# Earlier loads of the weight blocks in an attention-then-FFN kernel, with the squares in buffers of their own

## The chip, the core and the metric

The kernel runs on one core of a Trainium2 chip. The core has five engines that run their own instruction streams in order: TensorE (PE, with its weight loads shown as PEld), VectorE (DVE), ScalarE (ACT), GpSimd (POOL) and SyncE (SP), which here does nothing but issue DMAs. The metric is the device time of one execution in microseconds. The kernel before the change takes 992.15 us (median of three runs, 991.67 to 992.97).

## What is computed

Windowed causal attention with a linear bias, 8 batches of 8 heads, 576 positions, head size 64, window 128. Its output is the input of a bilinear feed-forward network with 512 model and 1536 hidden columns:

```
scores = scale * q @ k.T + bias        # only 0 <= i - j < 128 is kept
attn   = softmax(scores)
x      = (attn @ v), heads side by side  # 4608 x 512
out    = ((x @ w_a) * (x @ w_b)) @ w_out
```

All operands are float32, and the weights arrive as 64-bit words: the kernel takes them apart itself and turns each weight into a pair of float16 (high and low part), so that the large products run as three float16 products.

## The kernel before

**Stages.** Attention of batch 0 comes first (`first_attention`), in float32 and with the work on the weights woven in. Then, for each batch b, the feed-forward products of batch b ("up", lines 856 and 867 to 916; "down", lines 818 and 952) are woven with the attention of batch b+1 (`attention`, a generator that `Pace` advances). For batch 0 the functions are `first_up` and `first_down` (PE lines 856 and 818). Work on pairs of heads is called p0 to p3; the chain of a pair is scores (L380 or L384 on PE, L388 on DVE, L389 on ACT; in batch 0 L576, L587, L588), normalised probabilities `phl` (L405, L406), a transposing DMA into `pT` (L411; one buffer), and the product with v (L507).

**The weights.** 18 blocks pass through three places for raw data, `raws[n % 3]`, which lie in the storage of `wdn` (so the profile names them `wdn`). A block holds two slices: blocks 0 to 11 one of w_a and one of w_b, blocks 12 to 17 two of w_out. `load_weights` issues two DMAs of 512 KB on SP. `convert(n)` is three instructions on DVE that read the raw place and write the float32 form (L132, L134, L135; the form is named `wsum`). `squares(n)` is one ACT instruction (L141) that reads the form and writes the squares as bfloat16 **into the raw place of the same block**. For blocks 0 to 11 four matmuls on PE sum these squares (`up_norms`, L157, tile `wn_ps`), a reduction on DVE (L162) and three small POOL steps make the scales for two blocks, and `split_up` writes the float16 pairs `wup` (L149 on ACT, L150 on DVE). For blocks 12 to 17 ACT adds up the squares itself; when all six are done, L223, L102, one matmul (`wtot`, L103) and a few small steps make `ratio` (L227), with which L231 and L232 write the float16 pairs `wdn` over the raw places. A place can be loaded again only when the squares in it have been read, so `up_weights` puts the load of block f+3 behind the matmuls of block f, one turn of its loop after the conversion, and `down_weights` puts it behind the squares.

**What sets the order.** Python generators are advanced against each other: `other(...)` in `first_attention`, and `weave` in `first_batch`. That gives the order of the source; for PE, DVE, ACT and POOL a list scheduler then reorders up to the end of batch 0, by its own estimate of when operands are ready. SP's order is that of the source ("manual schedule"). From batch 1 on PE's order is that of the source too. On SP every DMA stands behind all that were issued before it: in `first_batch` the load of v for batch 1 (`load_v`, L273) waits until the last reader of v of batch 0 (L442) is done, and everything behind it on SP waits as well.

**Buffers that the change uses.** The pool `work` holds the tags "qk" (one buffer, 128 x 1152 float32) and "qst" (one buffer, 128 x 1152 float16). Both are first used for batch 2, by the loads at L316 and L317 and by L352 and L353.

## Time and profile before

| what | us |
|---|---|
| median of three runs (lowest, highest) | 992.15 (991.67, 992.97) |
| the profiled execution, its own time | 989.81 |
| the span of the profiled execution | 988.0 |
| PE busy in the span | 962.1 (97%) |
| DVE busy / ACT busy / POOL busy | 669.0 / 635.6 / 255.3 |

A row of the timeline begins with its start and its duration, both in us; durations overlap a little with the next row's start, because a row ends with the last write. Rows of the waits give the total, the number of times and the longest. The table of stretches gives, for each engine, the busy time and the number of instructions, then the granted PE clock, the share of the DMA engines and the rate.

### The profile page before, as it was taken

The page shows a single profiled execution, that of the slowest core. Times are in us where ns is not written, and L with a number is a line of the kernel's source. Part 1 is how long each engine was busy: PE and PEld are TensorE (multiplying, and loading weights), DVE is VectorE, ACT ScalarE, POOL GpSimd, SP SyncE. Part 2 cuts the span into 40 slices and gives each one's busy share as a digit, 9 for nine tenths or more (in the row PEclk, how much of TensorE's full clock was granted, in tenths as well). Part 3 has the DMA queues.
Part 4 walks back from the last instruction along what each step waited for, and adds up shares of the span by engine and source line. Part 5 has one row for each costly group of instructions (what it writes and reads, how often), then busy time and mean ns, then how long its engine had stood idle before and what let it go on. Part 6 is the DMA issues. An engine that isn't in the chain of part 4 may idle for free.

```text
span 988.0 us, 23867 instructions
## 1 busy us (share of the span) xinstructions
PE 962.1 (97%) x9339; PEld 748.9 (76%) x9339; DVE 669.0 (68%) x1867; ACT 635.6 (64%) x1729; POOL 255.3 (26%) x309
## 2 busy tenths in 40 slices
PE   7899999999999999999999999999999999999998
PEld 5567777677777777777777777777777777877776
DVE  5979998668688657777778677757776576514520
ACT  5977769667676667766767766777667766413321
POOL 1211122032546313541225222211232012311100
PEclk8999999999999999999999999999999999999999
DMA  8434753664337234463345362373245432200001
GB/s 333 168 126 172 231 154 67 151 158 92 80 74 183 68 69 87 107 172 75 68 92 121 120 118 65 87 191 84 59 84 117 133 74 38 55 34 5 1 13 36
DMA packets 148432, 102.82 MB, mean 104 GB/s; under 512 B 120032, under 2 KB 128352, under 8 KB 147296
## 3 DMA queue, kind: packets, MB, share of 16 engines
q1 hardware_dynamic: 138816, 91.77, 38.2%
q10 hardware_dynamic: 9504, 9.54, 3.0%
q8 instruction: 73, 1.20, 0.5%
q14 instruction: 39, 0.32, 0.1%
HBM read 48.33 MB, written 9.44 MB: 58 GB/s over the span
## 4 chain that ended last, share of the span: by engine, by line
PE 69%; DVE 12%; ACT 7%; DMA 7%; issue 3%; POOL 1%; SPq 0%; ACTq 0%; DVEq 0%
PE ch L856 19%; PE dn_ps L952 18%; PE p L856 14%; PE up_ps L856 9%; PE x_ps L507 4%; DMA v<-in_vP 4%; PE sc_ps L384 3%; DVE phl L406 2%; PE dn_ps L818 2%; ACT t L389 1%; DVE wsum L135 1%; DVE xs L442 1%; ACT phl L405 1%; DVE wsum L134 1%; DMA qk<-in_kT 1%
## 5 line engine op out<-in xcount | busy, mean ns | idle before, releaser
L856 PEld LDWEIGHTS <-wup 128*128 128x128 f16 x3072 | 296.3, 98 | 82.0 <-issue 5.7
L952 PE MATMUL dn_ps<-h,wdn 128*128 128x288 f16 x2016 | 254.4, 286 | 0.0
L952 PEld LDWEIGHTS <-wdn 128*128 128x128 f16 x2016 | 193.9, 98 | 52.0 <-issue 0.2
L856 PE MATMUL up_ps<-xs,wup 128*128 128x288 f16 x1536 | 194.6, 286 | 1.1 <-ACT rc L867 0.8
L856 PEld LDWEIGHTS <-wsum 128*128 128x128 f16 x1152 | 111.7, 98 | 32.0 <-issue 2.5
L911 POOL TENSOR_TENSOR rc<-rc,row 128x288 f32<-128x288 f32 x64 | 62.3, 974 | 279.8 <-DVE row L909 263.9
L389 ACT ACTIVATE t<-t,mn 128x192 f32<-128x192 f32 (+2 forms) x252 | 107.2, 427 | 24.5 <-DVE mn L388 24.4
L856 PE MATMUL ch<-xs,wup 128*128 128x288 f16 x768 | 115.0, 286 | 0.5 <-ACT row L893 0.5
L856 PE MATMUL p<-xs,wup 128*128 128x288 f16 x768 | 115.1, 286 | 0.0
L406 DVE SCALAR_TENSOR_TENSOR phl<-t,rin,phl 128x192 f16<-128x192 f32 (+2 forms) x252 | 104.6, 454 | 15.3 <-ACT phl L405 15.1
L856 PE MATMUL ch<-xs,wsum 128*128 128x288 f16 x768 | 111.5, 286 | 1.1 <-ACT rc L881 1.1
L848 ACT CAST h<-rc 128x576 f16<-128x576 f32 x96 | 64.1, 668 | 69.1 <-DVE rc L916 37.2
L405 ACT ACTIVATE phl<-t,rin 128x192 f16<-128x192 f32 (+2 forms) x252 | 88.9, 425 | 25.3 <-DMA pT<-phl 12.7
L849 DVE TENSOR_TENSOR h<-rc,h 128x576 f16<-128x576 f32 x90 | 69.5, 772 | 30.5 <-ACT h L848 29.7
L388 DVE CUSTOM_DVE_ANT_0 t<-sc_ps,bias,neg 128x192 f32<-128x192 f32 (+2 forms) x216 | 73.9, 389 | 7.6 <-PE sc_ps L384 7.5
L957 ACT ACTIVATE row<-dn_ps,oi 128x288 f32<-128x288 f32 x56 | 27.6, 493 | 55.9 <-PE dn_ps L952 55.9
L893 ACT ACTIVATE row<-ch,g 128x288 f32<-128x288 f32 x64 | 31.8, 497 | 48.9 <-PE ch L856 48.9
L442 DVE TENSOR_TENSOR xs<-v,xs 128x576 f16<-128x576 f32 x52 | 47.8, 935 | 21.4 <-ACT xs L441 21.3
L888 DVE TENSOR_TENSOR rc<-p,rc 128x288 f32<-128x288 f32 x64 | 29.1, 454 | 44.3 <-PE p L856 34.7
L365 POOL TENSOR_SCALAR bias<-rel_sb,ninv,sl_sb 128x192 f32<-128x192 f32 x24 | 20.0, 832 | 147.8 <-DVE mn L388 129.8
L856 PE MATMUL p<-xs,wsum 128*128 128x288 f16 x384 | 57.5, 286 | 0.0
L436 POOL TENSOR_TENSOR xq<-xq,sq 128x576 bf16<-128x576 bf16 x22 | 29.2, 1325 | 75.7 <-ACT sq L435 75.7
(155 smaller groups left out, 1386.1 us busy)
## 6 DMA issues: line engine op xcount, KB each, us to landing
v<-in_vP SPq DMA_DIRECT2D x8, 1280.0 KB, 6.2
out<-row ACTq DMA_DIRECT2D x62, 144.0 KB, 1.8
qk<-in_qT SPq DMA_DIRECT2D x28, 288.0 KB, 4.0
qk<-in_kT SPq DMA_DIRECT2D x28, 288.0 KB, 4.4
wdn<-in_w_a SPq DMA_DIRECT2D x12, 512.0 KB, 5.1
wdn<-in_w_b SPq DMA_DIRECT2D x12, 512.0 KB, 6.1
wdn<-in_w_out SPq DMA_DIRECT2D x12, 512.0 KB, 4.6
qst<-qkh SPq DMA_DIRECT2D x24, 144.0 KB, 2.7
```

Source lines behind the costliest of these rows:

```text
L388: vec.tensor_tensor_reduce(out=t[:, c:c + w], in0=ps[:, c:c + w], in1=o.bias[:, WIN - w:WIN], scale=-0.125 if o.b == 1 else o.neg, scalar= ...
L389: act.activation(t[:, c:c + w], t[:, c:c + w], AF.Exp, bias=o.mn[:, n:n + 1], scale=-1.0, accum_out=o.sm[:, n:n + 1])
L405: act.activation(phl[:, 0, pc:pc + w], e, AF.Copy, scale=s)
L406: vec.scalar_tensor_tensor(out=phl[:, 1, pc:pc + w], in0=e, scalar=s, in1=phl[:, 0, pc:pc + w], op0=ALU.mult, op1=ALU.subtract)
L442: vec.tensor_tensor(out=xs[:, n, 1, :, :], in0=src, in1=xs[:, n, 0, :, :], op=ALU.subtract)
L507: last = pe.matmul(xp[oc // 512][64 * h:64 * h + 64, o0:o0 + w], vt[0:rows, c:c + 64], probs(pt, rows, blocks, h), start=(n == 0 and first ...
L848: act.copy(h[:, f, :, 0, :], hid)
L849: eng.tensor_tensor(out=h[:, f, :, 1, :], in0=hid, in1=h[:, f, :, 0, :], op=ALU.subtract)
L856: pe.matmul(ps[:, 0:HT], w[:, wi, k, :], xs[:, b, xi, k, :], start=(first and n == 0), stop=(last and n == len(ks) - 1), skip_group_check= ...
L893: last_read[0] = last_main[0] = act.activation(mid, ch, AF.Copy, scale=st.g)
L911: pool.tensor_tensor(out=x0, in0=x0, in1=mid, op=ALU.mult)
L952: pe.matmul(ps[:, 0:HT], wdn[:, f, wi, e * P:(e + 1) * P], h[:, f, t, hi, :], start=(m == 0 and n == 0), stop=(m == NF - 1 and n == 2))
```

## The change

The squares are written to three buffers of their own, taken from the tags "qk" and "qst". With that a raw place is free as soon as its block is converted, and the load of block n+3 is put right behind the conversion of block n, in `up_weights` as in `down_weights`. In `first_batch` the generator of the weights is advanced four steps before the attention of batch 1 is started, which puts two blocks more in front of that batch's load of v on SP.

```
+    wsq = work.tile([P, 2, 2, DM], BF16, tag="qk", name="wsq")
+    wsq2 = work.tile([P, 2, DM], BF16, tag="qst", name="wsq2")
+    places = [wsq[:, 0], wsq[:, 1], wsq2]
 ...
     def squares(n, **kw):
-        sq = raws[n % 3].bitcast(BF16)[:, :, 0:512]
+        sq = places[n % 3]
 ...
+    def load_raw(n):
+        if n < NF:
+            load_weights(n, (w_a[n], w_b[n]), sp)
+        elif n < NF + NF // 2:
+            k = 2 * (n - NF)
+            load_weights(n, (w_out[k], w_out[k + 1]), sp)
 ...
     def up_weights():
                 up_norms(n, sq.pop(n), ps)
-                if n + 3 < NF:
-                    load_weights(n + 3, (w_a[n + 3], w_b[n + 3]), sp)
-                else:
-                    k = 2 * (n + 3 - NF)
-                    load_weights(n + 3, (w_out[k], w_out[k + 1]), sp)
             yield
             next(conv, None)
+            if f < NF:
+                load_raw(f + 3)
 ...
     def down_weights():
             next(conv, None)
+            if n < NF // 2:
+                load_raw(NF + n + 3)
             if n:
                 squares(NF + n - 1, accum_out=sums[:, n - 1:n])
-                if n + 2 < NF // 2:
-                    load_weights(NF + n + 2, (w_out[2 * n + 4], w_out[2 * n + 5]), sp)
 ...
     def first_batch():
         st = states[0]
+        for _ in range(4):
+            next(weights)
```

No instruction is added or removed on any engine; the scheduler and SP put them in another order. The places that the prediction speaks of follow. Lines of the changed kernel are numbered 3 higher from L90 on and 7 higher from L166 on, so that L132, L134, L135 (the three steps of a conversion) are L135, L137, L138 there, L610 and L611 are L617 and L618, and L442 is L449.

SP, from the last loads of `first_attention` to the load of v for batch 1. Before, the first q and k of batch 1 (L309, L310) stand behind block 2, with the loads of blocks 3 to 7 between them and v:

```order
L546 DMA qk_159<-in_qT 128x576
L547 DMA qk_159<-in_kT 128x576
L309 DMA qkh<-in_qT 128x576
L310 DMA qkl<-in_kT 128x576
L121 DMA wdn<-in_w_a 128x512
L121 DMA wdn<-in_w_b 128x512
```

In the change seven blocks, 3 to 9, stand there in a row, and then come, from block 9 on:

```order
L124 DMA wdn<-in_w_a 128x512
L124 DMA wdn<-in_w_b 128x512
L316 DMA qkh<-in_qT 128x576
L317 DMA qkl<-in_kT 128x576
L280 DMA v<-in_vP 128x2560
```

So ten blocks instead of eight are loaded ahead of v, and q and k of batch 1 stand behind all of them.

DVE, the end of `first_attention`: the last scores of batch 0 (ISA, `sc_ps`) and what follows up to the reciprocal for its fourth pair. Before:

```order
L587 ISA t,mn_688<-sc_ps,bias_476 128x192
L587 ISA mn_688 128x1
L132 TENSOR_SCALAR wsum<-wdn 128x1024
L442 TENSOR_TENSOR xs<-v,xs 128x576 x2
L134 SCALAR_TENSOR_TENSOR wsum<-wdn,wsum 128x1024
L610 TENSOR_SCALAR rin_707<-sm_569 128x9
L135 SCALAR_TENSOR_TENSOR wsum<-wdn,wsum 128x1024
L611 RECIPROCAL rin_707<-rin_707 128x9
```

In the change:

```order
L594 ISA t,mn_690<-sc_ps,bias_480 128x192
L594 ISA mn_690 128x1
L137 SCALAR_TENSOR_TENSOR wsum<-wdn,wsum 128x1024
L138 SCALAR_TENSOR_TENSOR wsum<-wdn,wsum 128x1024
L449 TENSOR_TENSOR xs<-v,xs 128x576 x2
L138 SCALAR_TENSOR_TENSOR wsum<-wdn,wsum 128x1024
L617 TENSOR_SCALAR rin_711<-sm_571 128x9
L618 RECIPROCAL rin_711<-rin_711 128x9
```

Ahead of the last scores stand, before, seven first, seven second and seven third steps of conversions; in the change ten, nine and eight. At the reciprocal eight conversions are complete before, ten in the change.

PE, around the one matmul `wtot`, late in `first_up`. Before, behind 556 of the 576 matmuls of `first_up` and one product with v of batch 1 (42 matmuls):

```order
L856 MATMUL up_ps<-xs,wup 128x288
L103 LDWEIGHTS ones_73
L103 MATMUL wtot<-c_1797,ones_73 128x1
L380 MATMUL sc_ps<-qkl,qkh 64x192 x4
L507 LDWEIGHTS vhl
L507 MATMUL x_ps<-pT,vhl 64x128
```

In the change, behind 503 of the 576 and ahead of the first product with v:

```order
L863 MATMUL up_ps<-xs,wup 128x288
L106 LDWEIGHTS ones_73
L106 MATMUL wtot<-c_1695,ones_73 128x1
L514 LDWEIGHTS vhl
L514 MATMUL x_ps<-pT,vhl 64x128
```

`wtot` moved forward past 53 matmuls of `first_up`, 42 of the product with v and one group of scores. From batch 1's own up products on, the order of PE, DVE and ACT is the same in both.

## The prediction

> **What bounds the kernel now.** I read the page's head, then PE's waits, then a table of stretches, then the timeline where PE waits.
>
> ```profile
> span 988.0 us, 23867 instructions
> PE 962.1 (97%) x9339; PEld 748.9 (76%) x9339; DVE 669.0 (68%) x1867; ACT 635.6 (64%) x1729; POOL 255.3 (26%) x309
> ```
>
> PE is idle for 988.0 - 962.1 = 25.9 us in all. The change alters no instruction and, from batch 1's up products on, no order; so only idle time of PE before that can move. The waits of PE over the span name three larger pieces:
>
> ```profile
> PE wtot L103 <- DVE c L102: 2.4, 1, 2.4
> PE x_ps L507 <- DMA pT<-phl: 2.4, 1, 2.4
> PE sc_ps L380 <- issue: 1.4, 1, 1.4
> ```
>
> All three lie in the up and down products of batch 0. The stretches (PE, PEld, DVE, ACT, POOL busy, PE clock, DMA) say who sets the pace in each:
>
> ```profile
> 10.00:20.00 10.00, 7.29 (x78) 5.43 (x78) 6.74 (x16) 8.54 (x25) 1.26 (x1) 0.66 1.02 399
> 30.00:40.00 10.00, 7.70 (x79) 5.17 (x79) 10.00 (x32) 9.83 (x31) 2.22 (x3) 1.00 0.58 208
> 40.00:50.00 10.00, 9.58 (x108) 6.12 (x106) 9.97 (x28) 9.94 (x30) 1.93 (x3) 1.00 0.26 88
> 50.00:60.00 10.00, 8.21 (x123) 5.91 (x119) 8.19 (x18) 8.02 (x20) 2.44 (x6) 1.00 0.06 22
> 60.00:70.00 10.00, 9.74 (x97) 7.05 (x97) 6.26 (x16) 6.01 (x17) 1.65 (x3) 1.00 0.32 113
> 70.00:80.00 10.00, 10.00 (x88) 7.22 (x85) 8.81 (x28) 8.02 (x26) 0.17 (x1) 1.00 0.93 353
> 80.00:90.00 10.00, 10.00 (x85) 7.87 (x84) 10.00 (x20) 6.80 (x14) 2.60 (x4) 1.00 0.44 162
> 140.00:150.00 10.00, 6.41 (x83) 4.93 (x81) 8.79 (x24) 7.52 (x18) 2.55 (x2) 1.00 0.25 59
> ```
>
> From 30 to 50 DVE has no idle time at all: the attention of batch 0 and the conversions share it, and DVE sets when the last scores are done. From 70 on PE is full. So a conversion step that is put ahead of batch 0's last scores costs its whole length, and one that is taken out of the stretch under PE gains only what PE waits for DVE there, in 140 to 150.
>
> **Part 1, the end of batch 0's attention.** By the order, three first steps (L132), two second (L134) and one third (L135) more stand ahead of the last scores. DVE's timeline gives what each takes, from its start to that of the next row:
>
> ```profile
> 43.83 0.68 DVE L132 TENSOR_SCALAR wsum<-wdn 128x1024 int32<-128x1024 int32 x1
> 44.43 0.35 DVE L587 CUSTOM_DVE_ANT_0 t<-sc_ps,bias 128x192 f32<-128x192 f32 x1
> 46.38 1.21 DVE L134 SCALAR_TENSOR_TENSOR wsum<-wdn,wsum 128x1024 int32<-128x1024 int32 x1
> 47.52 1.40 DVE L150 SCALAR_TENSOR_TENSOR wup<-wsum,sup,wup 128x512 f16<-128x512 f32 x2
> 50.24 1.22 DVE L135 SCALAR_TENSOR_TENSOR wsum<-wdn,wsum 128x1024 uint32<-128x1024 uint32 x1
> 51.38 0.35 DVE L587 CUSTOM_DVE_ANT_0 t<-sc_ps,bias 128x192 f32<-128x192 f32 x1
> 51.94 1.60 DVE L132 TENSOR_SCALAR wsum<-wdn 128x1024 int32<-128x1024 int32 x1
> 57.31 0.88 DVE L628 SCALAR_TENSOR_TENSOR v<-x_ps,sv,rin 128x512 f32<-128x512 f32 x2
> 62.50 0.94 DVE L628 SCALAR_TENSOR_TENSOR v<-x_ps,sv,rin 128x512 f32<-128x512 f32 x2 [4.32 <-PE x_ps L507]
> ```
>
> That is 3 x 0.60 + 2 x 1.14 + 1.14 = 5.2 us. Behind the last scores the change has 0.5 us more again (a third step in place of a first), and saves about 0.9: the first step at 51.94 lasts 1.60 instead of 0.68 because its block was still landing. At the next landmarks, the products with v of the third and fourth pair (57.31 and 62.50), the delay is between 4.3 and 5.7. The idle 4.32 us ahead of the last row are no cover, since the new steps stand ahead of them. PE has the same work before this point in both orders, so all of the delay is idle time on PE, which has no other work there: the up products need these v. I take **+4.4**, near the lower end, since ACT loses only one L141 and may catch up.
>
> The loads themselves can add to it. A conversion waits in order for its block, and its block can be issued only when its place has been converted. The page gives the landing:
>
> ```profile
> wdn<-in_w_b SPq DMA_DIRECT2D x12, 512.0 KB, 6.1
> ```
>
> With 0.4 us for the DMA ahead of it that is 6.5 us from the free place to the data. Adding up DVE's rows between the last step of block n-3 and the first of block n in the new order gives 6.9, 6.5, 7.5 and 6.8 us for blocks 6 to 9. So the data just arrive; I book 0 and keep up to +3 for the range. The q and k of batch 1, now behind block 9, are issued near 49 and are needed on PE after 65: covered. The load of v (issued at 65.97 before) goes with the last L442, some 5 us later, as does its first reader; the blocks behind it on SP (10 to 17) are each needed over 5 us after they can land.
>
> More idle time on PE can cost clock as well. In 10 to 20 PE idles 2.7 us and the granted clock is 0.66; in 50 to 60 it idles 1.8 us and the clock is 1.00. The new 4.4 us fall beside the second stretch, spread over gaps around the late scores and products, so I book 0. [...]
>
> **Part 2, `wtot`.** By the order DVE has less to do between the last v of batch 0 and the last conversion: two conversions (5.8), one L301, two L794 and two L388. PE now comes to `wtot` earlier too:
>
> ```profile
> L856 PE MATMUL up_ps<-xs,wup 128*128 128x288 f16 x139 | 17.9, 286 | 0.0
> L507 PE MATMUL x_ps<-pT,vhl 128*64 128x128 f16 (+2 forms) x42 | 1.5, 229 | 0.0
> L232 DVE SCALAR_TENSOR_TENSOR wdn<-wsum,ratio,wdn 128x512 f16<-128x512 f32 x12 | 8.8, 792 | 0.2 <-ACT wdn L231 0.2
> L794 DVE SCALAR_TENSOR_TENSOR rc<-rc,g,up_ps 128x288 f32<-128x288 f32 x11 | 5.5, 499 | 0.4 <-ACT rc L792 0.4
> L406 DVE SCALAR_TENSOR_TENSOR phl<-t,rin,phl 128x192 f16<-128x192 f32 x11 | 4.1, 412 | 0.0
> L388 DVE CUSTOM_DVE_ANT_0 t<-sc_ps,bias 128x192 f32<-128x192 f32 x12 | 3.8, 347 | 0.0
> ...
> 159.05 0.88 DVE L301 SCALAR_TENSOR_TENSOR vhl<-v,sv,vhl 128x640 f16<-128x640 f32 x1
> ...
> 144.49 1.06 ACT L141 ACTIVATE wdn<-wsum 128x1024 bf16<-128x1024 f32 x1 [2.18 <-DVE wsum L135]
> 145.67 0.16 DVE L223 TENSOR_REDUCE wo<-wos 128x1 f32<-128x6 f32 x1 [0.72 <-ACT wdn L141]
> 146.11 0.15 DVE L102 CAST c<-wo 128x1 bf16<-128x1 f32 x1
> 146.32 0.18 PE L103 MATMUL wtot<-c,ones 128*128 128x1 bf16 x1 [2.44 <-DVE c L102]
> 146.43 0.87 PE L380 MATMUL sc_ps<-qkl,qkh 64*64 64x192 f32 x8
> 150.20 0.88 PE L380 MATMUL sc_ps<-qkl,qkh 64*64 64x64 f32 x12 [1.36 <-issue]
> ```
>
> A matmul of the up product takes 17.9 / 139 = 0.129 us; 53 of them, the product with v (1.5) and a group of scores (0.8) are 9.1 us. PE came to `wtot` at 146.32 - 2.44 = 143.9; now at 143.9 + 4.4 - 9.1 = 139.2. DVE's relief is 5.8 + 0.9 + 2 x 0.50 + 2 x 0.32 = 8.3 us. The last conversion ended at about 144.4, where L141 could begin; now at 144.4 + 4.4 - 8.3 = 140.5, and the squares and small steps up to `wtot` add 146.3 - 144.4 = 1.9 as before: 142.4, a wait of 3.2. DVE's idle time on the way (3.7 and 1.2 us in 60 to 80, of which 2.5 lie ahead of 62.50) may shrink, so I take a wait as long as before. The stall moves and does not go: **0**, with bounds of -2.4 (DVE early after all) and +1. The other wait, of the scores at 150.20 for a bank that DVE freed late, should go, since behind `wtot` DVE now has only L227 and the scales ahead of it: **-1.4**.
>
> **Part 3, the transposes of batch 1.** SP's rows and the landing time:
>
> ```profile
> 160.65 4.84 SPq L411 DMA_TRANSPOSE pT<-phl  x1
> 174.65 5.17 SPq L411 DMA_TRANSPOSE pT<-phl  x1
> pT<-phl SPq DMA_TRANSPOSE x28, 6.8
> ...
> 168.14 1.54 PE L507 MATMUL x_ps<-pT,vhl 128*64 128x128 f16 x42
> ```
>
> Seven of the nine L406 of p2 came ahead of L227 before, beside the wait for `wtot`; now all nine stand behind it, and with them two L232, four L794, four L388 and one L301 more: 7 x 0.37 + 2 x 0.73 + 4 x 0.50 + 4 x 0.32 + 0.9 = 8.2 us. Before, the transpose started 160.65 - 146.32 = 14.3 us behind `wtot`, of which 3.7 were L406 and others ahead of L227 that take about 1.2 now. With `wtot` at 142.4 or a little before it starts near 142 + 14.3 - 2.5 + 8.2 = 162 instead of 160.65, and near 164.5 if ACT's L405, which also moved back, are slower. With 6.8 it lands between 168.8 and 171.3. PE comes to the product with v (168.1 before) at 168.1 + 4.4 - 1.4 - 1.0 (eight down matmuls fewer ahead) = 170.1. I take **+1.0** of new wait, bounds 0 and +2. For p3 PE has 97 down matmuls between the two products instead of 76: 21 x 0.129 = 2.7 us more cover against the wait of 2.4. I take **-2.0**, bounds -2.4 and 0.
>
> **Sum.** 4.4 + 0 - 1.4 + 1.0 - 2.0 = +2.0 us. The profiled execution takes 989.8 (span 988.0), 2.3 less than the median of the runs shown; it would become 991.8, and the median **994.2**. A measurement of this kernel can tell about 0.2% (2 us) from no change, so the forecast lies on that edge.
>
> **Rivals.**
> - *The earlier conversions cost nothing, and the kernel is faster.* Place: DVE between 30 and 57. If the chain through ACT and PE (ACT is at 9.83 and 9.94 there) set the last scores and DVE found 5 us of idle time in the new order, part 1 would be 0 to 1, and the later parts would count: -1.4 - 2.0, and up to -2.4 at `wtot`. That is -2.4 to -5.8, some 988.5. It decides from 2.4 us of found idle time. Against it: DVE's 10.00 and 9.97. Chance 0.14.
> - *The gains balance the loss.* `c` is ready as PE comes to `wtot` (-2.4 there): 2.0 - 2.4 = -0.4, 991.7. For it: DVE's idle time between 62.5 and 80 came partly from late blocks, which are early now. Against it: the last square on ACT still stands between. Chance 0.24.
> - *The data come late.* Place: first steps of blocks 6 to 9 on DVE. Each waits 0.5 to 1 us in order, with the scores behind it: +2.5 more, 996.7. For it: the 1.60 us row above. Against it: the DMA share is 0.58 and 0.26 there. Chance 0.20.
> - *The change does nothing*, since v still blocks SP for later blocks: that holds for blocks 10 to 17 only; ten conversions ahead of v are in the order. It is part of the second.
> - *PE's clock falls* in one long gap near 60. A stretch like 10 to 20 would then cost the full PE behind it up to 10 x (1 - 0.66) = 3.4 us: 997.6. Against it: the 1.00 in 50 to 60. Chance 0.04. [...]
>
> **Chances.** The forecast itself gets 0.38, half of it beyond 0.2%. Slower: 0.19 + 0.20 + 0.04, and 0.02 of the second, 0.45. Within 0.2%: 0.19 + 0.20 + 0.02 = 0.41. Faster: 0.12 + 0.02 = 0.14. The likeliest case alone spans 992.5 to 996. The range leaves out most of the first rival and the far end of the third: 990.2 to 998.
>
> **What would show it.** Right: the last row of L587 starts near 56 (51.38 before), L628 of the fourth pair starts near 67 instead of 62.50, PE's busy time in 50 to 60 falls; `wtot` still waits 2 to 3 us for L102, near 142; no wait of L380 behind it; the wait for `pT` sits at p2's product, not p3's. Wrong: idle time on DVE between 32 and 57, L628 before 65, a `wtot` without a wait, or waits of L132 for its DMA of more than 1 us each.

## The result, and the profile after

The changed kernel takes 1001.52 us (median of six runs, 1000.9 to 1003.02) against 992.56 (989.5 to 995.0) for the kernel before beside it: ratio 1.0094, 95% interval 1.0076 to 1.0113. It is 9 us slower. The forecast was 994.2 with a range up to 998, so the side was right and the size was not.

The head of the page:

```profile
span 1000.2 us, 23837 instructions
PE 965.5 (97%) x9339; PEld 751.0 (75%) x9339; DVE 668.4 (67%) x1867; ACT 636.2 (64%) x1729; POOL 256.3 (26%) x309
```

DVE, ACT and POOL are as busy as before, within 1 us. PE is busy 3.4 us longer (965.5 against 962.1) with the same instructions, and idle 34.7 us instead of 25.9. The two profiled spans differ by 12.2 us, more than the medians: the execution that was profiled before (989.81) lay 2.7 us below its median, the one after (1001.99) 0.5 above. The waits of PE, with total, times and the longest:

```profile
PE x_ps L514 <- DMA pT<-phl: 9.1, 2, 6.8
PE tr_ps L601 <- ACT t L595: 6.1, 7, 1.5
PE x_ps L514 <- ACT rin L628: 3.4, 3, 1.7
...
PE wtot L106 <- DVE c L105: 0.4, 1, 0.4
```

The wait for `pT`, 2.4 us before, is now the largest, and one piece of it is 6.8 us long. `wtot`, forecast to wait 2.4 to 3.2 us, waits 0.4. The scores' wait at 150.20 (1.4 us before, put down to a bank by the forecast and to "issue" by the profile) is gone, as forecast. Three stretches of 10 us (PE, PEld, DVE, ACT, POOL busy, granted PE clock, DMA) show where time was lost, and the fourth is from the kernel before:

```profile
50.00:60.00 10.00, 5.58 (x69) 3.80 (x70) 10.00 (x23) 8.75 (x24) 1.50 (x1) 0.93 0.32 116
60.00:70.00 10.00, 9.74 (x112) 6.65 (x110) 4.97 (x11) 2.22 (x5) 1.27 (x5) 0.89 0.01 2
...
190.00:200.00 10.00, 4.09 (x53) 3.64 (x53) 3.67 (x11) 5.46 (x15) 0.00 (x0) 0.66 0.62 127
...
180.00:190.00 10.00, 7.57 (x100) 5.79 (x98) 5.54 (x19) 7.11 (x21) 0.10 (x1) 1.00 0.36 93
```

In 50 to 60 PE lost 2.6 us of busy time (8.21 before), while DVE has no gap. In 190 to 200 PE is busy 4.09 us, and the clock there is 0.66; before, the same wait lay in 180 to 190, with PE busy 7.57 us and the clock at 1.00. So there are two main places.

**The front.** DVE's timeline at the end of batch 0's attention, and then POOL's row beside it and PE's product with v; the last two rows are the last scores and the product before the change:

```profile
56.74 0.35 DVE L594 CUSTOM_DVE_ANT_0 t<-sc_ps,bias 128x192 f32<-128x192 f32 x1
...
57.02 1.22 DVE L137 SCALAR_TENSOR_TENSOR wsum<-wdn,wsum 128x1024 int32<-128x1024 int32 x1
58.16 2.30 DVE L138 SCALAR_TENSOR_TENSOR wsum<-wdn,wsum 128x1024 uint32<-128x1024 uint32 x1
...
69.06 0.94 DVE L635 SCALAR_TENSOR_TENSOR v<-x_ps,sv,rin 128x512 f32<-128x512 f32 x2 [5.00 <-PE x_ps L514]
...
57.88 1.50 POOL L443 TENSOR_TENSOR xq<-xq,sq 128x576 bf16<-128x576 bf16 x1 [12.17 <-ACT sq L442]
...
58.32 2.94 PE L514 MATMUL x_ps<-phl,v 128*64 128x128 f32 x20 [1.73 <-ACT rin L628]
...
51.66 0.35 DVE L587 CUSTOM_DVE_ANT_0 t<-sc_ps,bias 128x192 f32<-128x192 f32 x1
53.97 1.74 PE L507 MATMUL x_ps<-phl,v 128*64 128x128 f32 x20 [0.52 <-ACT rin L621]
```

The last scores are 5.1 us later (56.74 against 51.66 for the last row; the 51.38 of the prediction is the row before that), the last v of batch 0 6.56 us (69.06 against 62.50). The third conversion step at 58.16 takes 2.30 us instead of 1.22.

**Pair p3 of batch 1.** ACT, SP and PE after:

```profile
181.25 1.16 ACT L333 ACTIVATE qkl<-qk 128x1152 bf16<-128x1152 f32 x1 [4.47 <-DMA qk<-in_kT]
...
183.40 1.49 ACT L412 ACTIVATE phl<-t,rin 128x192 f16<-128x192 f32 x4 [0.46 <-DVE rin L409]
...
176.93 0.64 SPq L324 DMA_DIRECT2D qk<-in_kT  x1
186.37 5.70 SPq L418 DMA_TRANSPOSE pT<-phl  x1
...
173.23 1.54 PE L514 MATMUL x_ps<-pT,vhl 128*64 128x128 f16 x42 [2.29 <-DMA pT<-phl]
...
195.91 2.77 PE L514 MATMUL x_ps<-pT,vhl 128*64 128x128 f16 x42 [6.80 <-DMA pT<-phl]
```

and the same place before, ACT and PE:

```profile
172.65 1.49 ACT L405 ACTIVATE phl<-t,rin 128x192 f16<-128x192 f32 x4 [0.74 <-DVE rin L402]
176.86 1.16 ACT L326 ACTIVATE qkl<-qk 128x1152 bf16<-128x1152 f32 x1 [2.72 <-DMA qk<-in_kT]
...
183.93 1.54 PE L507 MATMUL x_ps<-pT,vhl 128*64 128x128 f16 x42 [2.44 <-DMA pT<-phl]
```

Two rows of ACT have changed places. Before, the last four rows that write p3's probabilities (L405) ran at 172.65, and the squares for the scale of batch 2's second pair (L326), which wait for a load, stood behind them. After, the squares (L333) stand ahead: they wait 4.47 us for a load that SP issued at 176.93, and the four rows (L412) begin at 183.40, 10.75 us later than before. The transpose is 11.7 us later (186.37 against 174.65), and PE stands 6.80 us for it.

### The profile page after: what moved, and what is told of

Its sections match the earlier page's. It is cut to its first block, busy times and chain, and to the rows that moved or that the text cites. A ratio compares the mean times of both kernels' runs of the same rounds, so it can differ in the third digit from the quotient of the medians.

```text
span 1000.2 us, 23837 instructions
## 1 busy us (share of the span) xinstructions
PE 965.5 (97%) x9339; PEld 751.0 (75%) x9339; DVE 668.4 (67%) x1867; ACT 636.2 (64%) x1729; POOL 256.3 (26%) x309
## 4 chain that ended last, share of the span: by engine, by line
PE 68%; DVE 13%; DMA 7%; ACT 7%; issue 3%; POOL 1%; SPq 0%; ACTq 0%; DVEq 0%
PE ch L863 19%; PE dn_ps L959 18%; PE p L863 14%; PE up_ps L863 9%; PE x_ps L514 4%; PE sc_ps L391 3%; DVE phl L413 2%; DMA v<-in_vP 2%; DMA pT<-phl 2%; DMA qk<-in_kT 1%; DVE xs L449 1%; DVE t L395 1%; DVE wsum L138 1%; PE dn_ps L825 1%; DVE wup L153 1%
## 5 line engine op out<-in xcount | busy, mean ns | idle before, releaser
L412 ACT ACTIVATE phl<-t,rin 128x192 f16<-128x192 f32 (+2 forms) x252 | 88.9, 426 | 28.3 <-DMA pT<-phl 14.6
L449 DVE TENSOR_TENSOR xs<-v,xs 128x576 f16<-128x576 f32 x52 | 47.7, 932 | 21.9 <-ACT xs L448 21.8
L895 DVE TENSOR_TENSOR rc<-p,rc 128x288 f32<-128x288 f32 x64 | 29.1, 455 | 44.1 <-PE p L863 34.7
L514 PE MATMUL x_ps<-pT,vhl 128*64 128x128 f16 (+2 forms) x1176 | 44.0, 232 | 9.1 <-DMA pT<-phl 9.1
```

The costliest lines, as they stand in the source:

```text
L412: act.activation(phl[:, 0, pc:pc + w], e, AF.Copy, scale=s)
L449: vec.tensor_tensor(out=xs[:, n, 1, :, :], in0=src, in1=xs[:, n, 0, :, :], op=ALU.subtract)
L514: last = pe.matmul(xp[oc // 512][64 * h:64 * h + 64, o0:o0 + w], vt[0:rows, c:c + 64], probs(pt, rows, blocks, h), start=(n == 0 and first ...
```

## The experiments

All ratios are against runs of the kernel before on the same chip, and given with their 95% intervals. The kernel before takes up to 1.5 us more on one chip than on another, so the ratios and not the medians are compared; a difference of two ratios is uncertain by about 1.5 to 2.5 us. The landmarks come from one profile of each kernel. In the expectations "last x_ps" is DVE's last v of batch 0, T2 and T3 are the transposes of p2 and p3, and `qtot` is the sum on PE from which a pair's scale is made.

| kernel | ratio (95%) | last v of batch 0, DVE | first transpose (p1) | transpose of p3 | PE's wait for p3's `pT` | load of v, batch 2 |
|---|---|---|---|---|---|---|
| before | 1 | 62.50 | 133.51 | 174.65 | 2.44 | 202.12 |
| changed | 1.0094 (1.0076, 1.0113) | 69.06 | 143.59 | 186.37 | 6.80 | 212.64 |
| squares_behind | 1.0040 (1.0024, 1.0056) | 69.12 | 143.96 | 180.94 | none | 207.18 |
| conv_behind | 1.0106 (1.0090, 1.0122) | 69.07 | 144.15 | 186.09 | 4.55 | 213.14 |
| both_behind | 1.0045 (1.0030, 1.0061) | 68.32 | 142.88 | 180.27 | 0.21 | 207.21 |
| front_sq | 1.0011 (1.0001, 1.0020) | 64.21 | 141.24 | 176.23 | none | 202.86 |
| four_steps_only | 1.0027 (1.0014, 1.0039) | 64.11 | 145.81 | 187.92 | none | 209.03 |
| places_only | 1.0016 (1.0005, 1.0027) | 67.78 | 137.90 | 178.46 | 1.09 | 204.41 |
| no_four_steps | 1.0077 (1.0062, 1.0091) | 67.32 | 136.54 | 180.42 | 5.09 | 209.67 |
| no_four_sq | 1.0016 (1.0003, 1.0028) | 68.68 | 137.46 | 177.53 | none | 204.60 |
| no_four_all | 0.9999 (0.9989, 1.0010) | 64.21 | 135.60 | 174.12 | none | 201.58 |
| wtot_back | 1.0033 (1.0022, 1.0043) | 68.54 | 133.82 | 172.64 | none | 203.11 |
| all_back | 1.0009 (0.9999, 1.0019) | 64.43 | 134.02 | 172.79 | none | 202.57 |
| all_back6 | 1.0053 (1.0035, 1.0071) | 64.69 | 138.07 | 175.63 | none | 205.06 |
| hoist_alone | 1.0023 (1.0012, 1.0035) | 63.02 | 134.00 | 181.28 | 3.96 | 206.29 |
| places_front | 0.9986 (0.9975, 0.9996) | 64.12 | 134.42 | 174.98 | 2.06 | 202.82 |
| no_pool_sum | 1.0095 (1.0078, 1.0113) | 68.41 | 143.50 | 185.59 | 4.78 | 211.35 |
| places_front_np | 0.9968 (0.9955, 0.9981) | 64.14 | 134.38 | 174.94 | 1.44 | 201.28 |

### 1. The order on ACT at p3, taken back

`tc.issue_after(x)` keeps an instruction behind `x` on its own engine; the row held so, at 181.34 below, waits 0.92 us and for its load alone. `last_norm` is the last row that writes probabilities.

```
-            act.activation(phl[:, 0, pc:pc + w], e, AF.Copy, scale=s)
+            last_norm[0] = act.activation(phl[:, 0, pc:pc + w], e, AF.Copy, scale=s)
 ...
-            with behind():
+            with behind(), tc.issue_after(last_norm[0].ins) if i == NPAIR else ExitStack():
                 nxt = squares(i + 1)
```

> The changed kernel with one edit: the squares of the query-key block of batch 2's second pair on ACT stand behind the last four rows that write pair 3's probabilities, as before the change, instead of ahead of them. Theory A (that row waited 4.47 us for its load and held pair 3's probabilities, transpose and product with v; PE then stood 6.80 us and its clock fell): the last four L412 rows start near 177 to 178 instead of 183.40, T3 near 180.5 instead of 186.37, PE's wait for pair 3's pT falls from 6.8 to between 0.5 and 2.5 us, the time to 994 to 996.5. Rival B (T3 is late because T2 and all ahead of it are 5 us late, so that the order on ACT only shows where the lateness is spent): less than 1.5 us come back, 1000 to 1001.5. Rival C (the squares, now behind, hold the next pair's scale, for which PE waits in its fixed order): pair 3's wait goes but a wait of 2 us or more for batch 2's qtot takes its place, 997 to 999.

A span of 992.9 us, ratio 1.0040: 5.4 us of the 9.3 are gone (0.0054 and 0.0094 x 992). ACT, then SP:

```profile
178.94 1.49 ACT L412 ACTIVATE phl<-t,rin 128x192 f16<-128x192 f32 x4 [0.45 <-DVE rin L409]
181.34 1.16 ACT L333 ACTIVATE qkl<-qk 128x1152 bf16<-128x1152 f32 x1 [0.92 <-DMA qk<-in_kT]
...
180.94 5.28 SPq L418 DMA_TRANSPOSE pT<-phl  x1
```

The squares run when they ran in the changed kernel (181.34 against 181.25), since their load sets that. The probabilities and the transpose are 4.5 and 5.4 us earlier, and PE does not wait for p3 at all. Theory A holds, though the four rows came 1 us later than it said; B falls by the time, and C because the waits for `qtot` are 1.4 and 0.7 us as in the changed kernel. One thing more moved: on PE 84 down matmuls instead of 97 now stand between the products of p2 and p3. On the second base (experiment 3) their number stays at 99 with and without this edit, and the gain is 6.1 us.

### 2. The conversions, held back at the front

In the first form, the eighth and later blocks are converted behind the last scores; alone, and together with the edit above.

```
+        with tc.issue_after(last_score[0].ins) if n >= 7 else ExitStack():
             vec.tensor_scalar(out=t, in0=high, scalar1=3, ...)
 ...
-                vec.tensor_tensor_reduce(out=e, in0=ps[:, c:c + w], in1=biases[p]...
+                last_score[0] = vec.tensor_tensor_reduce(out=e, ...
```

> The changed kernel with one edit: the weight blocks from the eighth on may be converted on DVE only behind the last scores of batch 0, so that seven blocks stand ahead of them as before the change (the change has ten begun and eight ended there). Theory A (the front is late by the DVE work ahead of these scores): the last row of the scores is back from 56.74 to 51.5 to 52.5, batch 0's last product with v ends near 61 to 62 instead of 67.1; the blocks are then converted later, the wait for wtot near 142 grows from 0.4 to 2 to 3.5 us, so that only 2.5 to 4 us of the 6.5 are left by batch 0's down, and pair 3's wait stays: 997 to 999.5. Rival B (the front is late by POOL's or ACT's rows or by the clock and not by DVE): the last x_ps stays behind 65, time 1001 to 1002. Rival C (the order behind it settles to the old one and all is regained): 993 to 995.

> Both edits of the two runs beside it in one kernel: what is left of the change is the squares' own places, the earlier loads and more conversions between the last scores and batch 0's end. Theory A (the two causes add): the time of the changed kernel less both gains, 990.5 to 993.5, which is the kernel before or up to 2 us below it. Rival (a third cost of the change, in its loads or its four earlier steps, is still there): 995 to 998.

Neither moved the time (1.0106 beside 1.0094, 1.0045 beside 1.0040), so theory A of both missed. The two times lie near those of the rivals, but not for the rivals' reasons. DVE's timeline of conv_behind says why:

```profile
54.68 0.35 DVE L595 CUSTOM_DVE_ANT_0 t<-sc_ps,bias 128x192 f32<-128x192 f32 x1
...
62.04 1.21 DVE L139 SCALAR_TENSOR_TENSOR wsum<-wdn,wsum 128x1024 uint32<-128x1024 uint32 x1
...
69.07 0.94 DVE L636 SCALAR_TENSOR_TENSOR v<-x_ps,sv,rin 128x512 f32<-128x512 f32 x2 [2.63 <-PE x_ps L515]
```

The scheduler put seven of the nine held steps between the last scores and the reciprocal on which the last product rests, and the other two behind it, so all ten conversions still stood ahead of the last v, and it came at 69.07 as before the edit. The edit did not undo what it was meant to undo. In the second form the ninth and later blocks stay behind the last v of batch 0, too, as in the kernel before; the order on ACT is that of experiment 1.

```
+        with tc.issue_after((last_score if n < 8 else last_x)[0].ins) if n >= 7 else ExitStack():
```

> The changed kernel with the squares of batch 2's second pair behind pair 3's probabilities, and on DVE the eighth block's conversion behind batch 0's last scores and the ninth and later ones behind its last product with v, as before the change (the run with the eighth and later ones behind the scores alone left all ten ahead of that product, and batch 0's last x_ps at 69.07). Rival E (the front's delay by conversions is what is left over): last scores near 51.7, last x_ps near 62.5 to 64 instead of 69.1, and at least 2.5 us less than with the squares alone: 991.5 to 994. Theory D (it is not, the front's time is lost again ahead of the later waits): 995.5 to 997.5.

```profile
53.75 0.35 DVE L595 CUSTOM_DVE_ANT_0 t<-sc_ps,bias 128x192 f32<-128x192 f32 x1
...
64.21 0.94 DVE L636 SCALAR_TENSOR_TENSOR v<-x_ps,sv,rin 128x512 f32<-128x512 f32 x2 [4.39 <-PE x_ps L515]
```

The last v is 4.9 us earlier than in squares_behind (64.21 against 69.12), though the last scores gained less than expected, and the ratio falls from 1.0040 to 1.0011: 2.9 us. Rival E holds. With both orders taken back 1.1 us are left of 9.3.

### 3. The change taken apart

Four steps only: the kernel before with `for _ in range(4): next(weights)` ahead of batch 0's up. Places only: the kernel before with `places`. No four steps: the changed kernel without those two lines.

> The kernel before with only the four steps of weights taken ahead of batch 0's up; buffers and loads as before. On DVE seven blocks stand ahead of the last scores as before; on ACT the squares of batch 2's second pair stand ahead of pair 3's last four probabilities as in the changed kernel. Theory A (the order on ACT is a cost by itself, and this edit alone makes it): the front is as before (last scores near 51.7), PE waits 3 to 6 us for pair 3's pT instead of 2.44, 994.5 to 998. Rival (the hoisted squares hurt only where their load is late, which comes from the front): pair 3's wait within 1 us of 2.44, 991.5 to 993.5.

> The kernel before with only the squares' own places: loads and steps as before. The order on PE and on ACT around wtot and pair 3 is that of before; on DVE one block more is begun ahead of the last scores. Theory D: no cost but the front's small shift, 991.5 to 993.5. Rival (places of their own alone let squares and conversions run ahead and cost what the change costs): 996 or more.

> The changed kernel without the four earlier steps: squares' places and earlier loads. On PE wtot stands behind pair 0's product as before, on DVE nine blocks are begun ahead of the last scores (ten in the changed kernel, seven before). Theory D (the four steps carry nearly all of it, through wtot's place): 992 to 995. Rival E (the front's conversions, so the loads and places, carry it): 998 to 1001.

Places alone cost 0.16%, the four steps alone 0.27%, and everything but the four steps 0.77%; the expectation for the last (992 to 995) missed. It had put nearly all of the cost on the four steps, through the place of `wtot`. But the scheduler puts the squares ahead of p3's last four probabilities in no_four_steps as well, and PE waits 5.09 us for p3. In four_steps_only the order is also that of the changed kernel, and p3's transpose comes at 187.92, yet PE has no wait for it: the 994.87 us lie in the range of that run's theory A, but not by the wait that theory named. PE stands at the scale of batch 2's pairs (`qtot`), which rests on the same late squares:

```profile
PE qtot L337 <- DVE both L329: 4.6, 3, 3.2
PE qtot L337 <- DVE g L529: 2.2, 1, 2.2
```

Before, the first of these waits was 1.4 in all, and the second was not there. So the four steps bring the order about, and so does the rest of the change without them; the places alone do not. places_only also shows how little of the front can reach the end: its last v comes 5.3 us later than before, and it is 1.6 us slower.

The same edit as in experiment 1, on the second base, and then the front held back as well:

> The changed kernel without the four earlier steps, and with the squares of batch 2's second pair behind pair 3's probabilities: a second base for the same single edit. Theory A (ACT's order at pair 3 is a cost of its own): PE's wait of 5.09 us for pair 3's pT falls below 2 us and the time from 999.07 to 993 to 996. Rival B (the wait shows a lateness that comes from ahead): 997.5 or more.

> The same, and the conversions held back on DVE as in the run that gave the front back (eighth block behind the last scores, ninth and later behind batch 0's last product with v). Theory E (the front costs 2 to 3 us by itself, whatever the steps): last x_ps back from 67.3 to between 62.5 and 64.5, 990.5 to 993. Rival: no gain over the run without the hold, 993 to 996.

1.0077 becomes 1.0016 (6.1 us), and then 0.9999 (1.7 us). Both causes show again on a base of other lateness, the second only just clear of the uncertainty (about 1.6 us).

Next, `wtot` was put back to its old place in the program with four empty steps ahead of it in `down_weights`; on PE the product with v of p0 then stands ahead of `wtot` again. The order on ACT came back with this by itself.

```
+        for _ in range(4):
+            yield
         sab = small.tile([P, NF], F32, tag="sab", name="sab", bufs=1)
```

> The changed kernel with one edit: four empty steps ahead of the sum over the down weights, so that this sum (wtot) keeps the place that it had in the program before the change, while loads, squares' places and conversions stay as changed. On PE the product with v of batch 1's pair 0 then stands ahead of wtot as before the change (in the changed kernel behind it), and on ACT pair 3's probabilities stand ahead of the squares of batch 2's second pair again without any other edit. Theory D (both costs come from wtot's place in the order): pair 1's transpose near 134 to 139 instead of 143.59, pair 3's wait at most 2.5 us, the v load of batch 2 at 202 to 205, 991 to 994.5, so 2 us or more below the 996.44 of the run that moved the squares alone. Rival E (what was left there is the front, 6.5 us later, which nothing here touches): 995 to 997.5.

The first transpose is back at 133.82 and p3's wait is gone: 1.0033. The 993.68 us lie in theory D's range, but on a chip where the kernel before takes 991.06; by the ratios the further gain over squares_behind is 0.7 us, within their intervals, so rival E fits, and the place of `wtot` itself, 10 us at the first transpose, is not shown to be worth anything. This edit also changed PE's order in batch 0's down (38 down matmuls between the products of p1 and p2 and 142 between those of p2 and p3, instead of 96 and 97), so it is no test of `wtot` alone. With the front held back, too:

> The changed kernel with all three orders put back: wtot's place by four empty steps, the squares behind pair 3's probabilities, the conversions held back. What remains of the change are places, earlier loads, and conversions that run earlier from batch 0's up on. Theory (the causes add: 1.0033 with wtot's place alone, less 2.9 us for the front): 990 to 992.5, pair 1's transpose near 132 to 135, the v load of batch 2 near 200 to 202.5. Rival (the front's gain is lost at the next wait, since wtot stood ready without a wait with the late front): 992.5 to 994.5.

> The same with one block more held back (the seventh behind the last scores, the eighth and later behind the last product with v), so that DVE has one conversion of about 3 us less ahead of batch 0's scores than the kernel before. Theory E (the front pays while wtot does not wait): last scores 1 to 3 us earlier than in the run beside it, 988 to 991. Rival (the conversions saved there come due at wtot): wtot's wait grows to 1.5 to 4 us, and the time stays within 1 us of the run beside it, 990 to 993.

1.0009, 2.4 us less. One block more held back made it slower, 1.0053, with runs from 992.39 to 1001.29, and both expectations missed. Its profiled execution (span 991.7) lies near the lower end; it has no wait for `wtot`, and shows the last scores 2.8 us earlier, but the last v no earlier (64.69) and the first transpose 4 us later. What the longer executions do was not traced and stays open.

### 4. The order on ACT alone

The kernel before, with the squares made ahead of the last `normalize` of p3 and its four rows put behind them:

```
+            if i == NPAIR - 1:
+                early = squares(i + 2)
             if o:
-                with behind():
+                with behind(), tc.issue_after(last_sq[0].ins) if i == NPAIR - 1 else ExitStack():
                     normalize(o)
 ...
-                nxt = squares(i + 1)
+                nxt = early if i == NPAIR else squares(i + 1)
```

> The kernel before with one order alone: on ACT the squares of batch 2's second pair ahead of the last four rows that write pair 3's probabilities. The load for these squares landed at 176.9 in the kernel before, where the four rows began at 172.65. Theory A (this order costs by itself): the four rows begin near 178, T3 goes from 174.65 to between 179.5 and 181, PE's wait for pair 3's pT from 2.44 to between 6 and 9 us, and the time rises by 4 to 7 us against the kernel before. Rival B (it costs only where all else is late already): less than 2 us.

```profile
177.74 1.16 ACT L326 ACTIVATE qkl<-qk 128x1152 bf16<-128x1152 f32 x1 [5.26 <-DMA qk<-in_kT]
...
178.90 1.48 ACT L405 ACTIVATE phl<-t,rin 128x192 f16<-128x192 f32 x4
...
181.28 5.65 SPq L411 DMA_TRANSPOSE pT<-phl  x1
...
190.28 2.77 PE L507 MATMUL x_ps<-pT,vhl 128*64 128x128 f16 x42 [3.96 <-DMA pT<-phl]
```

ACT and SP do what theory A said: the transpose is 6.6 us later. The time rises by only 0.23%, 2.3 us, between the two theories. The scheduler filled the gap on PE: 107 down matmuls of batch 0 stand between the products of p2 and p3 instead of 76, 31 x 0.129 = 4.0 us more work, and the wait grew from 2.44 to 3.96 and not to 8. So the order is a cost by itself, and its size goes with how far the wait grows: from 2.44 to 3.96 us here (2.3 us of time), from none to 5.09 between no_four_sq and no_four_steps (6.1 us), from none to 6.80 between squares_behind and the changed kernel (5.4 us); the last two are not apart by more than their uncertainty. The clock that fell with the gap comes on top: p3's product took 2.77 us here and in the changed kernel instead of 1.54 (last section). In the profile of hoist_alone it fell at p0, too, where the order is the old one (p0's product took 2.77 us instead of 1.62, behind a wait for `wtot` of 2.41), so a part of the 2.3 us may not be the order's. In the changed kernel 97 matmuls stand there, and the squares start 3.5 us later than here (181.25 against 177.74).

### 5. The price of the front without the rest, and POOL's row

places_front is places_only with the conversions held back as in front_sq.

> The kernel before with the squares' own places, and on DVE the eighth block's conversion held behind batch 0's last scores and later ones behind its last product with v. Theory E (places cost only by what they let run ahead at the front): last x_ps near 62 to 64 instead of 67.8, and the time of the kernel before within 0.1%, 1 to 2 us less than with places alone. Rival (a wait for wtot takes it back): within 0.5 us of places alone.

1.0016 becomes 0.9986: 3.0 us, more than the 1 to 2 expected, and 0.14% under the kernel before. With front_sq (2.9), no_four_all (1.7) and all_back (2.4) that is four bases on which the hold gives 1.7 to 3.0 us for 3.7 to 4.9 us at the last v.

no_pool_sum is the changed kernel with POOL's sum of squares in batch 0 replaced by two more matmuls on PE. DVE's order is the same row for row.

```
-            square_x(p, st, x, first if p == 2 else work if p == 3 else None)
+            square_x(p, st, x, first if p in (1, 2) else work if p == 3 else None)
 ...
-            sq = keep.tile([P, S], BF16, tag="sq", name="sq")
+            sq = work.tile([P, 2, VCOLS], BF16, tag="vhl", name="sq", bufs=2)[:, 0, 0:S] if p == 1 else keep.tile(...)
```

> The changed kernel without POOL's sum of squares (xq) of batch 0's second pair: its squares stay in a buffer of their own, and PE adds them in with two more matmuls. DVE's order is unchanged row for row. Theory P (POOL's two-input row stretches DVE's two-input row beside it): the third conversion step near 58.2 takes 1.22 us instead of 2.30, the last x_ps on DVE starts 0.7 to 1.3 us earlier than 69.06, and the time falls by 0 to 1.2 us, hidden partly by the later waits: 1000 to 1001.7. Rival (that step was long for another reason, a late operand): it stays above 2 us.

```profile
57.07 1.23 DVE L137 SCALAR_TENSOR_TENSOR wsum<-wdn,wsum 128x1024 int32<-128x1024 int32 x1
58.21 1.23 DVE L138 SCALAR_TENSOR_TENSOR wsum<-wdn,wsum 128x1024 uint32<-128x1024 uint32 x1
...
68.41 0.94 DVE L635 SCALAR_TENSOR_TENSOR v<-x_ps,sv,rin 128x512 f32<-128x512 f32 x2 [4.88 <-PE x_ps L514]
```

The step of 2.30 us takes 1.23, and the last v comes 0.65 us earlier, just under the 0.7 expected. Theory P holds for the step; the time does not move measurably (1.0095). The same edit in places_front:

> The kernel with the squares' own places and the conversions held back at the front, and in it the same removal of POOL's row. Theory P: no conversion step ahead of the last x_ps longer than 1.4 us, last x_ps 0.5 to 1.3 us earlier than 64.1, the time 989.5 to 991.5, equal to the version with the row or up to 1 us below it. Rival: two more matmuls and a later scale cost as much, 991 to 992.5.

989.0 us, ratio 0.9968 (0.9955 to 0.9981): the only version that is faster than both kernels by more than 0.2%. The reason is not the one expected. No step ahead of the last v was stretched there even with POOL's row, and the last v stays at 64.14. The two intervals overlap, so whether this edit gave anything over places_front is open.

## Why the prediction went wrong, point by point

| step | predicted | measured in the changed kernel |
|---|---|---|
| last scores | 5.2 later | 5.1 later |
| last v of batch 0 (part 1) | +4.4 (4.3 to 5.7) | +6.56 |
| wait for `wtot` (part 2) | 0, still 2.4 to 3.2 | -2.1, waits 0.37 |
| scores' wait behind `wtot` | -1.4 | -1.4, gone |
| wait at p2's product (part 3) | +1.0 (0 to 2) | +2.3 |
| wait at p3's product (part 3) | -2.0 (-2.4 to 0) | +4.4, and 1.2 by the clock |

At batch 0's first down matmul 3.05 us of the front's 6.56 are left (156.52 against 153.47), which is about 6.56 - 2.1 - 1.4. With 2.3 at p2, 4.4 at p3 and 1.2 for the clock there that makes 10.9 of the 12.2 us between the two profiled spans; the rest was not followed.

**The step that failed is p3 in part 3.** It booked a gain of 2.0 us at p3's product, where the runs show a loss. It counted PE's cover (97 down matmuls instead of 76) against the old wait, and took the transpose of p3 to be no later than the other work. What feeds this transpose was not followed on ACT, where the order of two rows had turned. The turned order alone is worth 5.4 us in the changed kernel (experiment 1), 6.1 on a second base and 2.3 in the kernel before; each was measured. Without it the changed kernel stands at 1.0040, some 996.5, inside the range. So the forecast side, slower, would have held without p3, and it was no luck; more than half of the 9 us, though, came from a wait that the forecast had taken to shrink.

**Part 1 had the right mechanism and too small a size.** DVE did set the last scores, to 0.1 us, and no first step of a conversion waited for its block, DVE being at 10.00 from 30 to 60. So neither "the earlier conversions cost nothing" nor "the data come late" happened. The booked saving of 0.9 us did not exist: the row of 1.60 us at 51.94 before was read as a block still landing. It lay beside POOL's sum of squares:

```profile
51.70 1.28 POOL L436 TENSOR_TENSOR xq<-xq,sq 128x576 bf16<-128x576 bf16 x1 [9.59 <-ACT sq L435]
```

In the changed kernel the same POOL row met another step, which took 2.30 (experiment 5 shows the cause for that one; for the 1.60 it follows by likeness). The rest came from PE's clock, below. Not all of it reaches the end, as the sum took it to: undoing 3.7 to 4.9 us at the last v gave 1.7 to 3.0 us.

**Part 2 was too cautious.** PE came to `wtot` at 141.5 and waited 0.37 us; the estimate had `c` ready at 142.4 and PE there at 139.2. PE came later than that by the front's extra delay, and DVE had finished a little earlier. The rival "the gains balance the loss" had this mechanism, and by itself it was right.

**p2 in part 3 was the right place and too small.** Its transpose started at 166.20, where the estimate had 162 to 164.5, and landed at 173.2 instead of 168.8 to 171.3; PE came at 170.9, near the 170.1 of the estimate, and waited 2.29 us instead of 1.0. Which row ahead of the transpose was slower than estimated was not traced.

**The clock was booked at 0 in part 1, with a rival at 0.04, and fell at both places.** At the front, in steps of 1 us:

```profile
53.00:54.00 1.00, 0.47 (x3) 0.20 (x2) 1.00 (x2) 1.00 (x6) 0.00 (x0) 1.00 0.19 74
54.00:55.00 1.00, 0.44 (x2) 0.20 (x2) 1.00 (x2) 1.00 (x4) 0.00 (x0) 1.00 0.00 0
...
57.00:58.00 1.00, 0.00 (x0) 0.00 (x0) 1.00 (x3) 1.00 (x3) 0.12 (x1) 1.00 0.00 0
58.00:59.00 1.00, 0.68 (x10) 0.68 (x12) 1.00 (x2) 1.00 (x5) 1.00 (x1) 0.85 0.00 0
59.00:60.00 1.00, 1.00 (x8) 0.64 (x6) 1.00 (x1) 0.27 (x2) 0.37 (x1) 0.50 0.00 0
...
61.00:62.00 1.00, 1.00 (x8) 0.58 (x4) 1.00 (x3) 0.00 (x0) 0.64 (x3) 0.50 0.00 0
62.00:63.00 1.00, 1.00 (x11) 0.47 (x9) 1.00 (x2) 0.00 (x0) 0.31 (x1) 0.94 0.00 0
```

The 20 matmuls at 58.32 took 2.94 us; the same 20 took 1.74 before. These 1.2 us and the 0.65 that POOL's row was worth at the last v are most of the 2.2 by which part 1 was short; the share of the clock is read from the rows and was not tried alone. There was no long gap, which the rival had asked for: up to 58.32 PE's longest wait at the front was 1.73 us. That gaps spread around the late scores and products would leave the clock at 1.00, as part 1 booked it, did not hold here (last section). In front_sq, with the conversions held back, the clock is 1.00 in every stretch from 46 to 70.

## What to carry to other kernels

When a scheduler may reorder, compare the new order on every engine that feeds a wait, not only on the engines the edit names: here the largest loss sat over 100 us behind the front, in two groups of ACT rows that changed places, one of which waits for a load. An instruction that waits for a DMA (4.47 us here) is better put behind the work of its engine that is ready; where a scheduler had put it ahead, an ordering edge repaired it here on two bases, for 5.4 and 6.1 us. A loss at one place of a long chain must be followed to the end before it is booked: 4.9 of the 6.6 us at the front, taken back, gave 2.9 at the end.

## What the hardware showed beside that

**DVE beside POOL.** All conversion steps that begin in the first 140 us of sixteen profiles (all but the last two runs), grouped by the POOL instruction that they overlap by over 0.2 us, show one pattern: the steps of a kind took the same time, to 0.15 us, but for some of those beside a POOL instruction with two inputs. The larger groups of first and third steps:

| step on DVE, beside on POOL | rows | shortest, median, longest (us) |
|---|---|---|
| first step, nothing | 216 | 0.67, 0.69, 0.70 |
| first step, the scale of `bias` (one input) | 20 | 0.69, 0.84, 0.85 |
| first step, sum `xq` (two inputs, 128x576) | 9 | 0.68, 1.79, 1.81 |
| third step, nothing | 182 | 1.16, 1.22, 1.23 |
| third step, the scale of `bias` (one input) | 37 | 1.21, 1.22, 1.23 |
| third step, `h` minus (two inputs, 128x576) | 28 | 1.21, 1.49, 2.31 |
| third step, sum `xq` | 3 | 2.29, 2.30, 2.31 |

The longest steps are longer by 1.1 us, nearly the time that they overlap with POOL's row (1.2 to 1.3). What sorts the rows of these profiles is which began first. Beside `h` minus and `xq` 33 steps were stretched, counting second steps too, and all 33 began behind POOL's row; none of the 26 that began ahead of it was (12 more began behind it and kept their time). At times POOL's row was the longer one instead: the `bias` rows beside those 37 third steps took 1.26 to 2.30 us, while the shortest of the kernel before took 0.42 to 0.50. The third step has two inputs and the first step one, and both were stretched, to 2.31 and 1.81 us. With POOL's row taken out, the third step of 2.30 us took 1.23 (experiment 5). Why the rows get longer was not shown.

**PE's clock fell without a long gap.** Up to 58.32 the longest wait of PE at the front was 1.73 us, and PE was busy 2.2 of the 5 us from 53 to 58; then the clock was 0.50 for some 3.4 us (0.85, 0.50, 0.50, 0.50 and 0.94 in the five steps of 1 us from 58 to 63). Other kernels passed the place with similar gaps at 1.00 (conv_behind: busy 2.44 of 4 us in 54 to 58). At p3 the gap was unbroken:

```profile
188.00:192.00 4.00, 1.11 (x10) 0.65 (x7) 0.84 (x9) 1.25 (x1) 0.00 (x0) 0.98 1.13 208
192.00:196.00 4.00, 0.09 (x3) 0.12 (x5) 1.36 (x1) 0.20 (x1) 0.00 (x0) 0.50 0.84 180
196.00:200.00 4.00, 4.00 (x53) 3.52 (x53) 2.26 (x10) 4.00 (x14) 0.00 (x0) 0.67 0.11 37
```

The product behind it took 2.77 us instead of 1.54. In hoist_alone the gap was 3.96 us, up to 190.28:

```profile
188.00:192.00 4.00, 1.72 (x24) 1.54 (x26) 1.36 (x6) 1.68 (x6) 0.00 (x0) 0.56 0.45 104
192.00:196.00 4.00, 4.00 (x43) 2.94 (x40) 2.17 (x8) 4.00 (x13) 1.32 (x2) 0.59 0.24 56
```

while the two gaps of 2.44 us before the change cost no clock (1.00 in every step of 1 us from 140 to 152 and from 180 to 190). Other profiles have gaps of that length and shorter that did, as at p2 in conv_behind, where the product took 2.75 us instead of 1.54:

```profile
173.35 2.75 PE L515 MATMUL x_ps<-pT,vhl 128*64 128x128 f16 x42 [1.95 <-DMA pT<-phl]
```

Gaps of 2.14 (both_behind) and 2.15 us (squares_behind) at p2, 2.41 at `wtot` in hoist_alone and 2.69 at the front of conv_behind were followed by a clock of 0.50, too; the 2.29 us at p2 of the changed kernel were not. So the length of a gap does not sort them: the clock fell behind unbroken gaps of 1.95 to 2.69 us but not behind those of 2.29 and 2.44, at the front with none above 1.73, and in the gaps of 6.80 and 3.96 us some 2.7 and 2.2 us after their start (worked out from the stretches above, at 0.50 from there on). What sets the clock was not shown. That the share of busy time counts is the author's estimate from the front (2.2 of 5 us there against 2.44 of 4 us in conv_behind), and no run here tried it.
